# Moving small work off the tensor engine in a fused memory-attention and MLP kernel: w1 in quarters, segment sums on VectorE, a 64-column memory guess, a split last output

## The chip, the cores and the metric

One core of one Trainium2 chip. The metric is the device time of one execution in microseconds (us), as a median over runs. Engine names below: PE is the tensor engine, PEld its weight loads, DVE is VectorE, ACT is ScalarE, POOL is GpSimd, SP is SyncE, which issues most of the DMAs here. The granted clock is the share of its full clock that PE was given, as the profile lists it. L300 means line 300 of the kernel that is spoken of. The two kernels number their lines differently; the few lines that matter are given for both.

## The reference, cut to what matters

Two branches run on a layer-normalised input `xn` (2048 tokens of 1024) and are added. Branch B is an MLP with gelu; branch A is attention with 32 heads over 64 segments of 32 tokens, in which 8 memory rows are handed from each segment to the next:

```python
mem = mem0                                   # 8 rows of 1024
for s in range(64):
    h = concat([mem, xs[s]])                 # 8 + 32 rows
    q, k, v = h @ Wq, h @ Wk, h @ Wv
    o = softmax(mask(q k / sqrt(128))) v @ Wo
    mem = o[:8]                              # the next segment's memory
    out.append(o[8:])
```

This is a chain of 64 steps. The kernel breaks it with a guess. The weights are so small that each softmax is nearly flat, so a memory row is nearly the mean of the segment's values. With `sum_s` the sum of segment s over its tokens (for s = 0 plus the sum of the 8 rows of `mem0`), the guess for the memory after segment s is `(sum_s / 40) @ Wv @ Wo`. All segments are then computed in parallel from the guess. At the end the memory rows that come out are compared with those guessed, 70 rows in all. If one row is off by more than 2^-7 in relative norm, the kernel runs the serial loop of 64 segments after all. The result is right in both cases; only the time differs.

## The kernel before: the parts that matter

Stage 1 (the first MLP product) normalises token tiles, transposes them and multiplies them with w1. Tiles below `NPE` are transposed by PE, the others by ScalarE (normalise) and a DMA transpose. The segment sums are 8 matmuls per tile with a 0/1 matrix of 4 columns:

```python
NPE = 8
...
load_x(0); load_x(1)
for c in range(2):                                     # w1 in halves
    nc.sync.dma_start(w1_sb[:, :, c*512:(c+1)*512], w1_v[:, :, c*512:(c+1)*512])
    load_x(c + 2)
...
def seg_sums(n, xn):                                   # L290
    ps = psum0.tile([P, KT, 4], F32, tag="xs")
    for k in range(KT):
        nc.tensor.matmul(ps[:, k, :], xn[:, k*P:(k+1)*P], segsum[:], start=True, stop=True)
    nc.scalar.copy(xsum[:, :, 4*n:4*n+4], ps[:])
```

The guess is cut into 24 units (8 of Wv, 8 of Wo, 8 of Wv again) that are pushed between the matmuls of the MLP. `mem_start` makes the operand `xb` of the first 8:

```python
def mem_start():
    ...                                                # ps9: mem0 transposed, and its row sum in column M
    nc.vector.tensor_tensor(t0[:], ps9[:, :, M:M+1], xsum[:, :, 0:1], op=ALU.add)
    nc.vector.tensor_copy(xb[:, :, 8:NQ], xsum[:, :, 1:NSEG])
    nc.vector.tensor_copy(xb[:, :, 0:8], t0[:].to_broadcast((P, KT, 8)))   # NQ = 71 columns

for tb in range(4):                                    # blocks of 512 tokens
    for f in range(28):
        ... 8 matmuls with w3 (L523), gelu on ScalarE
        if tb == 0 and f == 20:
            mem_start()
        if tb > 0 and f % 7 == 6:
            spec_step(depth)                           # run one unit
    for j in range(4):
        n = tb * 4 + j
        R1, xt = r1s.pop(n); load_r1(n + 1)            # residual tiles
        ... 56 matmuls with w4 (L548), VectorE adds R1
        if n == 15:
            while pending or units: spec_step(depth)
        elif n > 0:
            spec_step(depth)                           # one unit here too, in block 0 as well
```

## Time and profile before

| | before |
|---|---|
| median | 1530.0 us (1529.5 to 1530.5 in the 4 runs beside the change) |
| span of the profiled run | 1527.2 us |
| first matmul of stage 1 / of the w2 product / of the value projection | 9.5 / 75.1 / 542.6 us |
| last PE matmul starts | 1521.7 us, 5.5 us before the end |

The head of the profile page (busy us, share of the span, number of instructions):

```profile
span 1527.2 us, 24314 instructions
## 1 busy us (share of the span) xinstructions
PE 1512.6 (99%) x9810; PEld 810.3 (53%) x9883; DVE 530.1 (35%) x1131; ACT 506.8 (33%) x1155; POOL 178.8 (12%) x248
```

All waits of PE in the view of waits (engine, tile, line, then what it waited for: us in total, times, longest):

```profile
PE ps L300 <- DMA w_sb<-in_B_w_dram: 2.0, 1, 2.0
PE ps L283 <- DVE xn L264: 1.3, 1, 1.3
PE warm L317 <- DVE wz L311: 1.3, 1, 1.3
PE ps L292 <- DVE xnk L273: 0.7, 1, 0.7
PE ps L300 <- ACT xn2T L287: 0.2, 1, 0.2
PE pso L710 <- issue: 0.2, 1, 0.2
```

PE is never without work for long: the waits sum to 5.7 us, nearly all in the first 20. So time can only come from fewer PE instructions, from the start, or from the tail.

The PE timeline gives the prices (start, length, engine, line, instruction, count). A segment sum (L292) pushes the next matmul back by 24.96 - 24.75 = 0.21 us; a guess unit (L440) takes 243.45 - 242.42 = 1.03 us. The listed length of 1.20 us is longer, as it overlaps the next line by 0.17 us:

```profile
24.75 0.34 PE L292 MATMUL ps<-c_segsum_sb,xnk 128*128 128x4 bf16 x8
24.96 1.25 PE L300 MATMUL ps<-xn2T,w_sb 128*128 128x256 bf16 x10
...
242.42 1.20 PE L440 MATMUL ps<-xb,wt 128*128 128x71 bf16 x32
243.45 2.75 PE L523 MATMUL ps<-xn3T,w_sb 128*128 128x512 bf16 x12
```

And two lines of the view by source line (minimum, median and maximum length in ns, then first and last start in us), the matmuls of `mem_start` (L425), the first guess unit (L440):

```profile
L425 PE MATMUL ps<-c_eye_sb,m x8: 162/162/176, 166.5 to 166.7; 8*128 8x9 bf16 x8
...
L440 PE MATMUL ps<-xb,wt x256: 196/198/198, 203.0 to 295.9; 128*128 128x71 bf16 x128
```

### The profile page before, as it was taken

What the parts mean: (1) busy time and instruction counts of PE and PEld (TensorE: products, weight loads), DVE (VectorE), ACT (ScalarE), POOL (GpSimd) and SP (SyncE); (2) the same over time, 40 slices, a digit from 0 to 9 for tenths busy, and PEclk for the clock granted to TensorE, in tenths of its full rate; (3) what the DMA queues carried; (4) which work ended last, traced back from release to release, by engine and by line L of the source; (5) the groups of instructions that cost most, each with busy time, mean ns of one, the idle gap of its engine ahead of it and who ended that gap; (6) DMA issues with size and microseconds to landing.
All of it is one profiled execution on the core that took longest, in us unless ns stands there. A gap on an engine that the chain in (4) does not pass through costs nothing.

```text
span 1527.2 us, 24314 instructions
## 1 busy us (share of the span) xinstructions
PE 1512.6 (99%) x9810; PEld 810.3 (53%) x9883; DVE 530.1 (35%) x1131; ACT 506.8 (33%) x1155; POOL 178.8 (12%) x248
## 2 busy tenths in 40 slices
PE   8999999999999999999999999999999999999998
PEld 7844444444444444444466645654665555445554
DVE  8284010000210122211146624650664266426641
ACT  5533202103012011111156614650663266326620
POOL 5232020221211222100000010001000100010001
PEclk9999999999999999999999999999999999999999
DMA  8679543452352877632399947992997389728611
GB/s 252 186 221 308 208 158 118 142 183 90 115 176 80 213 259 255 223 123 82 125 242 247 235 133 183 234 244 74 229 251 187 106 222 227 183 80 203 177 46 51
DMA packets 287373, 270.03 MB, mean 177 GB/s; under 512 B 136875, under 2 KB 255040, under 8 KB 287000
## 3 DMA queue, kind: packets, MB, share of 16 engines
q1 hardware_dynamic: 265208, 185.79, 47.5%
q0 software_dynamic: 22048, 82.63, 15.5%
q8 instruction: 80, 1.31, 0.4%
q14 instruction: 37, 0.30, 0.1%
HBM read 190.98 MB, written 46.19 MB: 155 GB/s over the span
## 4 chain that ended last, share of the span: by engine, by line
PE 98%; DMA 1%; DVE 0%; issue 0%; ACT 0%; SPq 0%
PE ps L652 30%; PE ps L579 14%; PE pso L710 14%; PE ps L523 13%; PE ps L548 13%; PE ps L387 4%; PE ps L300 3%; PE psS L667 2%; PE psO L691 2%; DMA xt<-in_A_x_dram 1%; PE ps L474 1%; PE ps L837 1%; PE ps L440 1%; PE gps L454 1%; PE ps L292 0%
## 5 line engine op out<-in xcount | busy, mean ns | idle before, releaser
L652 PE MATMUL ps<-hTb,wt 128*128 128x396 bf16 (+3 forms) x2560 | 509.5, 343 | 0.0
L652 PEld LDWEIGHTS <-wt 128*128 128x128 bf16 x2560 | 234.2, 98 | 166.1
L710 PE MATMUL pso<-wo_sb,oX 128*128 128x512 bf16 x1001 | 223.4, 379 | 1.3 <-issue 0.2
L579 PE MATMUL ps<-wt,xT 128*128 128x512 bf16 x1004 | 220.1, 379 | 1.1
L523 PE MATMUL ps<-xn3T,w_sb 128*128 128x512 bf16 x896 | 195.7, 379 | 0.0
L548 PE MATMUL ps<-w_sb,h3T 128*128 128x512 bf16 x872 | 194.3, 379 | 1.2
L579 PEld LDWEIGHTS <-xT 128*128 128x128 bf16 x1024 | 100.2, 98 | 120.8
L524 ACT ACTIVATE h3T<-ps 128x512 bf16<-128x512 f32 x112 | 66.9, 597 | 292.1 <-PE ps L523 291.2
L710 PEld LDWEIGHTS <-oX 128*128 128x128 bf16 x1024 | 98.8, 98 | 115.3
L658 ACT CAST KT<-ps 128x396 bf16<-128x396 f32 (+3 forms) x160 | 82.3, 514 | 224.0 <-PE ps L652 222.5
L548 PEld LDWEIGHTS <-h3T 128*128 128x128 bf16 x896 | 86.8, 98 | 102.8
L523 PEld LDWEIGHTS <-w_sb 128*128 128x128 bf16 x896 | 86.8, 98 | 102.7
L673 DVE TENSOR_REDUCE sums<-sm 99x4 f32<-99x396 f32 (+2 forms) x176 | 97.6, 555 | 113.4 <-ACT sm L671 113.4
L669 DVE TENSOR_TENSOR sm<-psS,c_mask_reg_sb 99x396 f32<-99x396 f32 x160 | 91.3, 571 | 90.2 <-PE psS L667 89.7
L671 ACT ACTIVATE sm<-sm 99x396 f32<-99x396 f32 (+2 forms) x176 | 92.8, 527 | 71.6 <-DVE sm L669 70.9
L581 ACT CAST Vs<-ps 128x512 bf16<-128x512 f32 x64 | 37.4, 586 | 233.3 <-PE ps L579 169.2
L660 ACT ACTIVATE QT<-ps 128x396 bf16<-128x396 f32 (+3 forms) x160 | 84.2, 526 | 74.0 <-PE ps L652 54.1
L585 DVE CAST Vs<-ps 128x512 bf16<-128x512 f32 x64 | 44.3, 692 | 170.0 <-PE ps L579 157.1
L549 DVE TENSOR_TENSOR R<-ps,R 128x512 f32<-128x512 f32 x32 | 22.1, 692 | 232.0 <-PE ps L548 221.1
L679 DVE TENSOR_TENSOR Pn<-sm,rs 99x396 bf16<-99x396 f32 (+2 forms) x176 | 98.9, 562 | 6.3 <-DVE rs L675 0.5
L692 ACT CAST oX<-psO 128x384 bf16<-128x384 f32 (+1 forms) x176 | 82.4, 468 | 8.3 <-PE psO L691 7.8
L717 POOL DMA_DIRECT2D out_dram<-ot x30 | 16.4, 546 | 583.5 <-DVE ot L716 577.6
(118 smaller groups left out, 978.3 us busy)
## 6 DMA issues: line engine op xcount, KB each, us to landing
wt<-in_A_Wk_dram SPq DMA_DIRECT2D x78, 512.0 KB
wt<-in_A_Wq_dram SPq DMA_DIRECT2D x76, 512.0 KB
wt<-in_A_Wv_dram POOLq DMA_DIRECT2D x24, 1024.0 KB, 6.8
V_scratch<-Vs SPq DMA_DIRECT2D x32, 512.0 KB
V<-V_scratch SPq DMA_DIRECT2D x32, 384.0 KB
w_sb<-in_B_w_dram SPq DMA_DIRECT2D x9, 1024.0 KB
R_scratch<-x POOLq DMA_DIRECT2D x16, 512.0 KB, 3.9
R<-R_scratch SPq DMA_DIRECT2D x16, 512.0 KB
```

The lines of the kernel that those rows point to most:

```text
L523: nc.tensor.matmul(ps[:].rearrange("p (n t) -> p n t", t=P), w3_sb[:, k, f * P:(f + 1) * P], xn3T[tb][:, :, k, :], start=(k == 0), stop=(k ...
L548: nc.tensor.matmul(ps[:], h3T[:, f, j * P:(j + 1) * P], w4_sb[:, f, ch * 512:(ch + 1) * 512], start=(f == 0), stop=(f == FT - 1))
L579: nc.tensor.matmul(ps[:], xT[:, m4 * 4 + j, k, :], wv[:, k, :], start=(k == 0), stop=(k == KT - 1))
L652: nc.tensor.matmul(ps[:, :nb] if flat else ps[:, :nb].rearrange("p (t c) -> p t c", t=nt), w[:, k, hh * P:(hh + 1) * P], B["rhs"](k), star ...
L658: nc.scalar.copy(o, i)
L660: nc.scalar.mul(o, i, scale)
L669: nc.vector.tensor_tensor(sm[:T, :, :T], S3, t["mask"][:].unsqueeze(1).to_broadcast((T, 4, T)), op=ALU.add)
L671: nc.scalar.activation(e[:T, :, :T], sm[:T, :, :T], ACTF.Exp, scale=LN2)
L673: nc.vector.tensor_reduce(ss, e[:T, :, :T], axis=AX.X, op=ALU.add)
L679: nc.vector.tensor_tensor(Pn[:T, :, :T], e[:T, :, :T], rs[:T, :].unsqueeze(2).to_broadcast((T, 4, T)), op=ALU.mult)
L692: nc.scalar.copy(oX[:, hs_, at:at + nt], O3[:, :, 0:nt])
L710: nc.tensor.matmul(self.ps[:], self.oX[:, h, self.gl * P:(self.gl + 1) * P], wo_sb[:, h, self.cc], start=(h == 0), stop=(h == H - 1))
```

## The change

The intent, in four parts: (1) start earlier, with w1 in four column quarters, and take the transposes of tiles 4 to 7 off PE (`NPE = 4`); (2) take the 128 segment-sum matmuls off PE: reload `xn` from its DRAM scratch with DMA transposes while w3 runs, and sum on VectorE; (3) compute the guess on 64 columns, not 71, as the first 8 are equal; (4) produce the last output tile in two halves of 256 columns, so that less is left to evict after the last matmul.

```diff
-                    NPE = 8
+                    NPE = 4
@@ start
                     load_x(0)
-                    load_x(1)
-                    for c in range(2):
-                        w1 half c; load_x(c + 2)
-                    for n in range(4, 7):
+                    for c in range(4):
+                        w1 quarter c
+                        if c < 2:
+                            load_x(c + 1)
+                    for n in range(3, 7):
                         load_x(n)
@@ warm-up matmuls: 13 -> 15; norm_stats(1, 0) now after norm2(0)
@@ MLP phase: the PE version of seg_sums is gone, and
+                def seg_sums(n):
+                    xr = ring.tile([P, KT, P], BF16, tag="xr")          # 2 buffers
+                    nc.sync.dma_start_transpose(xr[:], xn_v[:, n, :])
+                    nc.vector.tensor_reduce(xb[:, :, 4*n:4*n+4], xr[:]..., axis=AX.X, op=ALU.add)
                 def mem_start():
                     ...
-                    nc.vector.tensor_tensor(t0[:], ps9[:, :, M:M+1], xsum[:, :, 0:1], op=ALU.add)
-                    nc.vector.tensor_copy(xb[:, :, 8:NQ], xsum[:, :, 1:NSEG])
-                    nc.vector.tensor_copy(xb[:, :, 0:8], t0[:].to_broadcast((P, KT, 8)))
+                    nc.vector.tensor_tensor(xb[:, :, 0:1], ps9[:, :, M:M+1], xb[:, :, 0:1], op=ALU.add)
@@ in the loop over blocks
-                        if tb == 0 and f == 20:
+                        if tb == 0 and f >= FT - NT:
+                            seg_sums(f - FT + NT)
+                        if tb == 1 and f == 0:
+                            m0s = [ring.tile([M, D], BF16, tag="xr", name="m0")]
+                            nc.sync.dma_start(m0s[0][:], A_mem0[0])
+                        if tb == 1 and f == 3:
                             mem_start()
@@ guess units: NQ -> NSEG columns; GT rows 0 to 6 are copies of column 0; 72 -> 71 in the third set
@@ outputs: the last Out of 512 columns becomes two of 256; the last three stores go to the SP queue
```

More of the change, by code (lines that the diff above doesn't have):

```diff
@@ L125 @@
     ident = const_tile("c_ident", np.eye(P, dtype=np.float32))
-    segsum_np = np.zeros((P, 4), np.float32)
-    for t in range(P):
-        segsum_np[t, t // SEG] = 1.0
-    segsum = const_tile("c_segsum", segsum_np)
     eye9 = const_tile("c_eye9", np.concatenate([np.eye(M, dtype=np.float32), np.ones((M, 1), np.float32)], 1))
@@ L192 @@
             w3ctx = bctx.enter_context(ExitStack())
-            xctx = bctx.enter_context(ExitStack())
-            xsum = xctx.enter_context(tc.tile_pool(name="xs", bufs=1)).tile([P, KT, NSEG], BF16)
             w3_pool = w3ctx.enter_context(tc.tile_pool(name="w3", bufs=1, side="right"))
@@ L228 @@
                     load_x(0)
-                    load_x(1)
-                    for c in range(2):
-                        nc.sync.dma_start(w1_sb[:, :, c * 512:(c + 1) * 512], w1_v[:, :, c * 512:(c + 1) * 512])
-                        load_x(c + 2)
-                    for n in range(4, 7):
+                    for c in range(4):
+                        nc.sync.dma_start(w1_sb[:, :, c * 256:(c + 1) * 256], w1_v[:, :, c * 256:(c + 1) * 256])
+                        if c < 2:
+                            load_x(c + 1)
+                    for n in range(3, 7):
                         load_x(n)
@@ L287, in transposes @@
                             nc.scalar.copy(xn2T[:, jj, half * 4:half * 4 + 4, :], ps[:])
-                    def seg_sums(n, xn):
-                        ps = psum0.tile([P, KT, 4], F32, tag="xs")
-                        for k in range(KT):
-                            nc.tensor.matmul(ps[:, k, :], xn[:, k * P:(k + 1) * P], segsum[:], start=True, stop=True)
-                        nc.scalar.copy(xsum[:, :, 4 * n:4 * n + 4], ps[:])
                     def stage1(n0, nt, xn2T, between):
@@ L315 @@
                     ps = psum.tile([P, 512], F32, tag="mm", bufs=4, name="warm")
-                    for i in range(13):
-                        nc.tensor.matmul(ps[:], wz[:, :P], wz[:], start=(i == 0), stop=(i == 12))
+                    for i in range(15):
+                        nc.tensor.matmul(ps[:], wz[:, :P], wz[:], start=(i == 0), stop=(i == 14))
                     norm_stats(0)
-                    norm_stats(1, 0)
                     t0 = xn2T_tile()
                     xn2 = norm2(0, t0, 0)
+                    norm_stats(1, 0)
                     transposes(xn2, t0, 0, 0)
@@ L333, in first @@
                         transposes(xn2, t1, 0, 1)
-                    xns = {}
-                    def sums_of(n):
-                        if n in xns:
-                            seg_sums(n, xns.pop(n))
                     stage1(0, 1, t0, {3: [first], 4: [lambda: norm_stats(3)]})
@@ L349, in prep @@
                         for m in done:
-                            xns[m] = norm1(m)
+                            norm1(m)
                     def tr(n, half):
@@ L370 @@
                             between[5] += [lambda m0=m0: prep(m0 + 1)]
-                        between[3] += [lambda n0=n0: sums_of(n0 - 1)]
-                        between[4] += [lambda n0=n0: sums_of(n0 - 2)]
                         stage1(n0, nt, tiles2[n0], between)
-                    for n in range(NT):
-                        sums_of(n)
                 xn3T = [wpool.tile([P, 4, KT, P], BF16, tag="w", name=f"xn3T{tb}") for tb in range(4)]
@@ L410 @@
                 w4_sb = big.tile([P, FT, D], BF16)
-                m0 = ring.tile([M, D], BF16, tag="m0", bufs=1)
-                nc.sync.dma_start(m0[:], A_mem0[0])
                 for _ in range(4):
@@ L416 @@
                     nc.sync.dma_start(w4_sb[:, 4 * c:4 * (c + 1), :], w4_v[:, 4 * c:4 * (c + 1), :])
-                vbT = big.tile([P, H, NQ + 1], BF16)
-                xb = big.tile([P, KT, NQ + 1], BF16)
+                vbT = big.tile([P, H, NSEG], BF16)
+                xb = big.tile([P, KT, NSEG], BF16)
                 gps = []
+                def seg_sums(n):
+                    xr = ring.tile([P, KT, P], BF16, tag="xr")
+                    nc.sync.dma_start_transpose(xr[:], xn_v[:, n, :])
+                    with nc.allow_low_precision(reason="sums are accumulated in fp32 and rounded once"):
+                        nc.vector.tensor_reduce(xb[:, :, 4 * n:4 * n + 4], xr[:].rearrange("p k (s t) -> p k s t", t=SEG), axis=AX.X, op=ALU.add)
                 def mem_start():
+                    m0 = m0s[0]
                     ps9 = psum3.tile([P, KT, M + 1], F32, tag="vr")
@@ L426, in mem_start @@
                     nc.vector.tensor_copy(MZ[:, :, 0:M], ps9[:, :, 0:M])
-                    t0 = ring.tile([P, KT, 1], F32, tag="t0", bufs=1)
-                    nc.vector.tensor_tensor(t0[:], ps9[:, :, M:M + 1], xsum[:, :, 0:1], op=ALU.add)
-                    nc.vector.tensor_copy(xb[:, :, 8:NQ], xsum[:, :, 1:NSEG])
-                    nc.vector.tensor_copy(xb[:, :, 0:8], t0[:].to_broadcast((P, KT, 8)))
+                    nc.vector.tensor_tensor(xb[:, :, 0:1], ps9[:, :, M:M + 1], xb[:, :, 0:1], op=ALU.add)
                 def unit_vb(hg):
@@ L436, in run @@
                     def run():
-                        ps = psum3.tile([P, 4, NQ], F32, tag="vr")
+                        ps = psum3.tile([P, 4, NSEG], F32, tag="vr")
                         for hh in range(4):
                             for k in range(KT):
-                                nc.tensor.matmul(ps[:, hh, :], wv[:, k, hh * P:(hh + 1) * P], xb[:, k, :NQ], start=(k == 0), stop=(k == KT - 1))
-                        nc.vector.tensor_scalar(vbT[:, hg * 4:(hg + 1) * 4, :NQ], ps[:], 1.0 / L, None, op0=ALU.mult)
+                                nc.tensor.matmul(ps[:, hh, :], wv[:, k, hh * P:(hh + 1) * P], xb[:, k, :], start=(k == 0), stop=(k == KT - 1))
+                        nc.vector.tensor_scalar(vbT[:, hg * 4:(hg + 1) * 4, :], ps[:], 1.0 / L, None, op0=ALU.mult)
                     return run
@@ L449, in run @@
                         if c == 0:
-                            gps.extend(psum3.tile([P, 4, NQ], F32, tag="g", name=f"gps{i}") for i in range(2))
+                            gps.extend(psum3.tile([P, 4, NSEG], F32, tag="g", name=f"gps{i}") for i in range(2))
                         for hh in range(4):
@@ L453, in run @@
                             for k in range(KT):
-                                nc.tensor.matmul(gps[k // 4][:, k % 4, :], wo[:, hh, k * P:(k + 1) * P], vbT[:, h, :NQ],
+                                nc.tensor.matmul(gps[k // 4][:, k % 4, :], wo[:, hh, k * P:(k + 1) * P], vbT[:, h, :],
                                                  start=(h == 0 and k % 4 == 0), stop=(h == H - 1), skip_group_check=True)
@@ L457, in run @@
                             for i in range(2):
-                                nc.vector.tensor_copy(GT[:, 4 * i:4 * i + 4, :], gps[i][:])
+                                nc.vector.tensor_copy(GT[:, 4 * i:4 * i + 4, 7:NQ], gps[i][:])
+                                nc.vector.tensor_copy(GT[:, 4 * i:4 * i + 4, 0:7], gps[i][:, :, 0:1].to_broadcast((P, 4, 7)))
                             nc.vector.tensor_copy(MZ[:, :, M:NQ + 1], GT[:, :, 7:NQ])
@@ L473, in run @@
                             for k in range(KT):
-                                nc.tensor.matmul(ps[:, hh, :NQ + 1], wv[:, k, hh * P:(hh + 1) * P], MZ[:, k, :], start=(k == 0), stop=(k == KT - 1))
+                                nc.tensor.matmul(ps[:, hh, :NQ], wv[:, k, hh * P:(hh + 1) * P], MZ[:, k, :NQ], start=(k == 0), stop=(k == KT - 1))
                         vrs = vrs2[hg % 2]
-                        nc.vector.tensor_copy(vrs[:, :, :NQ + 1], ps[:, :, :NQ + 1])
+                        nc.vector.tensor_copy(vrs[:, :, :NQ], ps[:, :, :NQ])
                         vrt = ring.tile([P, 4, P], BF16, tag="vrt")
                         nc.sync.dma_start_transpose(vrt[:], vrs[:].rearrange("p h r -> p (h r)"))
-                        nc.sync.dma_start(Vr_d[:, hg * 512:(hg + 1) * 512].rearrange("r (h e) -> r h e", e=DH), vrt[:NQ + 1])
+                        nc.sync.dma_start(Vr_d[:NQ, hg * 512:(hg + 1) * 512].rearrange("r (h e) -> r h e", e=DH), vrt[:NQ])
                     return run
@@ L557 @@
                         nc.gpsimd.dma_start(R_v[:, n, :], R1[:])
-            xctx.close()
             vsp = vctx.enter_context(tc.tile_pool(name="vsp", bufs=3, side="right"))
@@ L698, with __init__ @@
         class Out:
-            def __init__(self, oX, gi, gl, ch):
-                self.oX, self.gi, self.gl, self.cc, self.ps = oX, gi, gl, slice(ch * 512, (ch + 1) * 512), None
+            def __init__(self, oX, gi, gl, c0, w=512):
+                self.oX, self.gi, self.gl, self.cc, self.ps, self.w = oX, gi, gl, slice(c0, c0 + w), None, w
                 self.late = self.last = False
@@ L707, in piece @@
                     self.Rt = iop.tile([P, 512], F32, tag="Rt")
-                    nc.gpsimd.dma_start(self.Rt[:], R_v[:, self.gi, self.cc])
+                    nc.gpsimd.dma_start(self.Rt[:, :self.w], R_v[:, self.gi, self.cc])
                 for h in range(4 * hg, 4 * hg + 4):
-                    nc.tensor.matmul(self.ps[:], self.oX[:, h, self.gl * P:(self.gl + 1) * P], wo_sb[:, h, self.cc], start=(h == 0), stop=(h == H - 1))
+                    nc.tensor.matmul(self.ps[:, :self.w], self.oX[:, h, self.gl * P:(self.gl + 1) * P], wo_sb[:, h, self.cc], start=(h == 0), stop=(h == H - 1))
                 if hg == 7:
@@ L713, in piece @@
                     if DEBUG_A:
-                        nc.vector.tensor_copy(ot[:], self.ps[:])
+                        nc.vector.tensor_copy(ot[:, :self.w], self.ps[:, :self.w])
                     else:
-                        nc.vector.tensor_tensor(ot[:], self.ps[:], self.Rt[:], op=ALU.add)
-                    (nc.sync if self.last else nc.gpsimd).dma_start(out_v[:, self.gi, self.cc], ot[:])
+                        nc.vector.tensor_tensor(ot[:, :self.w], self.ps[:, :self.w], self.Rt[:, :self.w], op=ALU.add)
+                    (nc.sync if self.last else nc.gpsimd).dma_start(out_v[:, self.gi, self.cc], ot[:, :self.w])
         smalls = []
@@ L810 @@
                     smalls.append((due, ("S", gi_), s_item))
-            outs = [Out(oXs[B["b"]], 3 * B["b"] + gl, gl, ch) for B in Bs for gl in range(4 if B["b"] == 4 else 3) for ch in range(2)]
+            outs = [Out(oXs[B["b"]], 3 * B["b"] + gl, gl, ch * 512) for B in Bs for gl in range(4 if B["b"] == 4 else 3) for ch in range(2)]
+        o = outs.pop()
+        outs += [Out(o.oX, o.gi, o.gl, c0, 256) for c0 in (512, 768)]
         head, rest = outs[:4], outs[4:]
@@ L816 @@
             o.late = True
-        for o in rest[-2:]:
+        for o in rest[-3:]:
             o.last = True
```

## The prediction

> **What bounds the kernel.** The tensor engine: PE is busy 1512.6 of 1527.2 us (page, part 1), and 98% of the chain of waits is PE. Its waits in all: 1.3 us for the first memset, 1.3 for the first normalised tile (L283), 2.0 for w1 (L300), 0.7 for the first segment sum (L292). After the last matmul (about 1522.1) some 5 us of eviction and store follow. Only removed PE instructions, the start and the tail can pay. VectorE is 35% busy, but 4.8 of each 5 us from 15 to 30 us (windows).
>
> **Costs, from start-to-start times in the PE timeline.**
> - Segment sums: 8 matmuls of 4 columns take 0.205 us (25.6 ns each), 16 times: 3.3 us removed. The replacement, 16 DMA transposes and 16 VectorE reductions (about 1.2 us each, estimated from 0.555 us for 396 elements), falls at 145 to 175 us, where VectorE is idle (3.1 of 50 us busy): free.
> - Transposes of tiles 4 to 7 leave PE: 8 matmuls of 56 ns per tile, 1.8 us.
> - Memory guess: 32 matmuls of 71 columns take 1.03 us (32.2 ns each). [...]
> - Last output: eviction of 256 instead of 512 columns, 0.69 to about 0.37 us, a smaller last store; short matmuls cost 0.1 us more. Net 0.4 us.
> - Start: 0.75 instead of 1.5 MB lie ahead of the first L300 matmul, so the 2.0 us wait should mostly vanish, with part of the slow clock (mean 0.66 from 10 to 15 us). But x1 now lies behind a w1 quarter and delays VectorE[...]; and x3 still lies behind 3 MB (it arrived at 13.56 us), and tile 2 is normalised only after x3's statistics (about 16 us). The early gain is mostly lost by then.
>
> **The new wait.** Tiles 4 and 5 now go through ScalarE and a DMA transpose on the SP queue. In program order tile 5's transpose stands behind the loads of x9 to x11, which wait for the kept copies of tiles 2 to 4 on VectorE (about 24.3 us by present durations); with 0.75 us per load and 1.3 us per transpose issue it lands at about 28.5 us. PE would be ready for group (4,5) at about 26.8 us: a wait of 1 to 2 us on xn2T. Before, that group started at 28.9 us. So almost nothing is gained until there; after it the remaining sums and transposes are won: 4.3 us for stage 1 as a whole (5.1 us removed and 3 us of start waits shortened, the rest given back in the new wait).
>
> **Sum.** 4.3 + 1.6 + 0.4 = 6.3 us: 1523.8 us, 0.4% faster. 8 in 10: 1520.0 to 1527.0. Faster by over 2%: 0.01; within: 0.98; slower: 0.01.
>
> **What would show it.** Right: L300's wait for w1 below 1 us; a PE wait on xn2T at 26 to 29 us; first L387 matmul at about 71 instead of 75.1 us; a guess unit 0.94 instead of 1.03 us; no PE wait at the new reductions; last matmul to end 0.4 us shorter. Wrong: no wait at group (4,5) and L387 at 68 to 69 us (total about 1521), or over 4 us of wait there (about 1526).
>
> **What would make it wrong.** Transposes landing late among the w2 and x loads; [...]the scratch transposes delaying MLP loads; the memory guess failing its check, which runs the serial loop (far slower).

Cut above is what did not come from the traces of this case: two clauses, and the working of one term of the sum, the 1.6 us for the guess units. The sum was 4.3 + 1.6 + 0.4 = 6.3 us, its 1.6 made of 1.5 us for 64 instead of 71 columns and 0.1 us for the third set. The profile of before gives the same 1.5 us (estimate): 56 matmuls of 256 columns take 70.58 - 64.47 = 6.11 us (L300), 109.1 ns each, against 32.2 ns at 71 columns, so 0.416 ns a column, 2.9 ns for 7 columns, 512 times. The other sizes beside what the profiles show: four transposes start to start 0.22 us (L283), 55 ns each. A reduction of 1024 elements, forecast at 1.2 us, took 1.22 us in the changed kernel (L404). The eviction of 256 columns, forecast at 0.37 us, took 0.42 us in the changed kernel (L703).

## The result, and the profile after

The changed kernel takes 7310.8 us (7307.8 to 7317.1, 4 runs), against 1530.0 for the kernel before in the same rounds: 4.78 times, interval 4.77 to 4.79. The result is correct. Here and below a ratio is the mean time of one kernel's fast runs over that of the other's of the same rounds, so not quite the ratio of the medians.

The head of the page, and two groups of its fifth part (busy us, mean ns | idle before and releaser):

```profile
span 7314.9 us, 134351 instructions
...
PE 5489.9 (75%) x58141; PEld 3019.1 (41%) x58141; DVE 1568.5 (21%) x3194; ACT 1220.1 (17%) x3055; POOL 179.5 (2%) x252
...
L905 PE MATMUL ps<-wv,hseg 128*40 128x512 bf16 x4096 | 1418.2, 509 | 163.0 <-DMA wv<-in_A_Wv_dram 163.0
L940 PE MATMUL ps<-wo_sb,oTs 128*40 128x512 bf16 x4096 | 1154.2, 430 | 33.0 <-ACT oTs L934 33.0
```

L905 and L940 lie inside the serial loop. It ran: the check of the guess failed. The windows before and after the end of the main part (length, then busy us of PE, PEld, DVE, ACT and POOL with their counts, granted clock, DMA share, GB/s):

```profile
0.00:1542.00 1542.00, 1515.12 (x9757) 807.80 (x9757) 545.93 (x1144) 505.63 (x1135) 179.50 (x252) 1.00 0.67 178
1542.00:7314.00 5772.00, 3974.74 (x48384) 2211.28 (x48384) 1022.60 (x2050) 714.42 (x1920) 0.00 (x0) 0.77 0.90 283
```

So 5772 us are the loop, and the main part ends at about 1542 us, not at the 1524 predicted. There are two things to explain, a large one and a small one. These lines answer to the two source lines of before, `mem_start` (L410 now) and the first eight units (L422 now):

```profile
L410 PE MATMUL ps<-c_eye_sb,m x8: 162/162/175, 254.2 to 254.4; 8*128 8x9 bf16 x8
...
L422 PE MATMUL ps<-xb,wt x256: 192/193/242, 218.4 to 312.7; 128*128 128x64 bf16 x128
```

Before, `mem_start` preceded the first unit by 36 us. Now it follows it by 36 us, and the PE timeline has three units ahead of it, at 218.4, 233.3 and 246.3 us. Each covers 4 heads, so heads 0 to 11 read column 0 of `xb` without the sum of `mem0`.

The waits of PE in the main part, longest first:

```profile
PE ps L422 <- DVE xb L404: 11.1, 1, 11.1
PE ps L288 <- DMA xn2T<-xn: 4.3, 2, 2.7
PE ps L566 <- ACT Vs L568: 2.6, 1, 2.6
PE ps L288 <- ACT xn2T L281: 2.5, 3, 1.9
PE ps L277 <- DVE xn L258: 2.4, 3, 1.1
...
PE ps L288 <- DMA w_sb<-in_B_w_dram: 0.6, 1, 0.6
```

The wait for w1 shrank from 2.0 to 0.6 us, as predicted. New are 11.1 us of the first unit for the VectorE sums (L404) and some 7 us in stage 1 (the lines of L288). Two of these waits cost more than their length, since the granted clock fell with them: 0.57 from 24 to 28 us (the 1.9 us for L281), 0.50 from 218 to 222 us. After the two for DMA transposes (2.7 and 1.6 us) it was 1.00. The w2 product starts at 79.3 us instead of 75.1; I had said 71.

Why the sums are late is in the SP queue's timeline:

```profile
157.84 2.92 SPq L393 DMA_DIRECT2D w_sb<-in_B_w_dram  x1
160.80 2.58 SPq L497 DMA_DIRECT2D R<-R_scratch  x1
163.43 0.43 SPq L498 DMA_DIRECT2D xr<-in_A_x_dram  x1
163.90 51.05 SPq L402 DMA_TRANSPOSE xr<-xn_scratch  x16
215.01 0.57 SPq L497 DMA_DIRECT2D R<-R_scratch  x1
```

The 16 transposes stand in program order behind the loads of w3, w4 (L393) and of the first residual tile. They are issued from 163.9 us on, and take 51.05 / 16 = 3.2 us each on average. That is no pure transpose time: the view of the queue's waits has 26.3 us of waiting in it, 11.7 of them until VectorE freed one of the two buffers. The sums end here (VectorE timeline; the 1.22 us each are as estimated):

```profile
175.78 2.35 DVE L404 TENSOR_REDUCE xb<-xr 128x32 bf16<-128x1024 bf16 x2 [39.08 <-DMA xr<-xn_scratch]
...
217.09 1.22 DVE L404 TENSOR_REDUCE xb<-xr 128x32 bf16<-128x1024 bf16 x1 [0.64 <-DMA xr<-xn_scratch]
```

The last ends at 218.3, the unit starts at 218.36. The load of the second residual tile (L497, at 215.01) also stands behind the 16 transposes; that will matter below.

### The profile page after: what moved, and what is told of

It reads as the page before. It is cut to its first block, busy times and chain, and to the rows that moved or that the text cites. A ratio compares the mean times of both kernels' runs of the same rounds, so it can differ in the third digit from the quotient of the medians.

```text
span 7314.9 us, 134351 instructions
## 1 busy us (share of the span) xinstructions
PE 5489.9 (75%) x58141; PEld 3019.1 (41%) x58141; DVE 1568.5 (21%) x3194; ACT 1220.1 (17%) x3055; POOL 179.5 (2%) x252
## 5 line engine op out<-in xcount | busy, mean ns | idle before, releaser
L905 PE MATMUL ps<-wv,hseg 128*40 128x512 bf16 x4096 | 1418.2, 509 | 163.0 <-DMA wv<-in_A_Wv_dram 163.0
L940 PE MATMUL ps<-wo_sb,oTs 128*40 128x512 bf16 x4096 | 1154.2, 430 | 33.0 <-ACT oTs L934 33.0
L906 DVE CAST Va<-ps 40x512 bf16<-40x512 f32 x512 | 349.6, 683 | 3057.7 <-PE ps L905 3057.7
L905 PEld LDWEIGHTS <-hseg 128*40 128x40 bf16 x4096 | 482.0, 124 | 874.7 <-issue 467.0
L896 PE MATMUL ps<-hseg,wq 128*128 128x40 bf16 x16384 | 558.5, 189 | 367.1 <-DMA wq<-in_A_Wq_dram 366.6
L901 PE MATMUL ps<-hseg,wk 128*128 128x40 bf16 x16384 | 525.5, 184 | 405.3 <-DMA wk<-in_A_Wk_dram 403.6
L896 PEld LDWEIGHTS <-wq 128*128 128x128 bf16 x16384 | 504.6, 103 | 519.6 <-issue 381.2
L901 PEld LDWEIGHTS <-wk 128*128 128x128 bf16 x16384 | 471.1, 98 | 520.4 <-DMA wk<-in_A_Wk_dram 449.7
L940 PEld LDWEIGHTS <-oTs 128*40 128x40 bf16 x4096 | 403.2, 111 | 506.8 <-issue 221.2
L697 PE MATMUL pso<-wo_sb,oX 128*128 128x512 bf16 (+1 forms) x1056 | 225.2, 373 | 0.0
L566 PE MATMUL ps<-wt,xT 128*128 128x512 bf16 x1024 | 221.3, 379 | 2.6 <-ACT Vs L568 2.6
```

Source lines behind the costliest of these rows:

```text
L566: nc.tensor.matmul(ps[:], xT[:, m4 * 4 + j, k, :], wv[:, k, :], start=(k == 0), stop=(k == KT - 1))
L697: nc.tensor.matmul(self.ps[:, :self.w], self.oX[:, h, self.gl * P:(self.gl + 1) * P], wo_sb[:, h, self.cc], start=(h == 0), stop=(h == H - 1))
L896: nc.tensor.matmul(ps[:, hh, :], wq[:, k, hh * P:(hh + 1) * P], hseg[:, k, :], start=(k == 0), stop=(k == KT - 1))
L901: nc.tensor.matmul(ps[:, hh, :], wk[:, k, hh * P:(hh + 1) * P], hseg[:, k, :], start=(k == 0), stop=(k == KT - 1))
L905: nc.tensor.matmul(ps[:L, :], hseg[:, k, :], wv[:, k, :], start=(k == 0), stop=(k == KT - 1))
L906: nc.vector.tensor_copy(Va[:, cs_], ps[:L, :])
```

## The experiments

### Why the loop runs: four kernels

Theory ORDER: the three early units read column 0 too soon. Rival ROUNDING: the 32-term sum with a bf16 output is not accumulated in fp32 as the code's comment claims, so many rows miss the tolerance. The rival is a serious one. I emulated the guess and one attention pass on the reference's own inputs, on a host, in three ways, and compared the relative distance of guessed and resulting memory rows with the tolerance 2^-7 = 0.0078:

```
variant                                          first memory's rows   largest other   rows failing
sums exact, then bf16                            0.0037                0.0036          0
sums accumulated in bf16                         0.0079                0.0084          21
sums exact, heads 0 to 11 without sum(mem0)      0.0160                0.0036          8
```

Both theories make the check fail, but with 8 and with 21 failing rows. (The emulation is no run on the chip. Its 0.0079 lies just above the tolerance, so the 21 is soft; the 0.0160 of the 8 rows is twice the tolerance.) This gives a test on the chip: the number of failing rows, plus a count of softmax sums that are out of range, is what the branch reads.

**mem_first.** The three units are held back to block 1.

```diff
-                        elif n > 0:
+                        elif tb > 0:
                             spec_step(depth)
```

> The changed kernel with one word altered: the three guess units that ran between the output tiles of the first token block are held back to the second block, so that the sum of the initial memory is added to column 0 before any unit reads it. Theory ORDER (three units, heads 0 to 11, read column 0 without the initial memory; the check then fails and the serial loop runs): no loop, about 1525 to 1533 us, and the 11.1 us wait of the guess matmuls for the reductions is gone. Rival ROUNDING (the 32-term sum with a bf16 output is accumulated in bf16, so many rows miss the tolerance): the loop still runs, about 7300 us.

Measured: 1577.3 us (1570.5 to 1584.8, 4 runs), ratio 1.029 (1.026 to 1.032); correct. No loop, with the VectorE sums unchanged: ROUNDING falls. But the time is 44 us above the upper end of what I expected. The longest wait of PE in its profile is

```profile
PE ps L566 <- ACT Vs L568: 37.0, 1, 37.0
```

at the turn to the value projection. That is taken up below.

**before_late.** The kernel before, with only the addition of `mem0` moved behind the three units. (`xb` is filled with the sums at the old place, since otherwise the units would read a tile that nobody has written; a memory check before the run refuses that. In the changed kernel the VectorE sums write column 0, so the tile is written and the check has nothing to say: the value is only incomplete.)

```diff
                         if tb == 0 and f == 20:
-                            mem_start()
+                            nc.vector.tensor_copy(xb[:, :, 8:NQ], xsum[:, :, 1:NSEG])
+                            nc.vector.tensor_copy(xb[:, :, 0:8], xsum[:, :, 0:1].to_broadcast((P, KT, 8)))
+                        if tb == 1 and f == 3:
+                            mem_start()
```

> The kernel before, its segment sums still by the tensor engine in fp32, with only the addition of the initial memory moved behind the first three guess units. ORDER: the serial loop runs, about 7310 us. ROUNDING: the sums are those of before, so no loop, about 1530 us.

Measured: 7282.9 us (one run). The order alone produces the loop, with sums by the tensor engine.

**count_over_8** and **count_over_7.** The changed kernel, with another threshold of the branch.

```diff
-    with tc.If(cond > 0):
+    with tc.If(cond > 8):        # count_over_7: cond > 7
```

> The changed kernel as it is, but the loop runs only when more than 8 of the 70 memory rows fail. ORDER: exactly the 8 rows of the first memory are wrong (an emulation of the arithmetic on a host gives 8 failing rows at twice the tolerance), so no loop; the time is that of the changed kernel's main part, about 1543 us, which the profile of the changed kernel shows ending near 1542 us. The result may be slightly wrong, on purpose. ROUNDING: the emulation gives 21 failing rows, so the loop runs, about 7310 us.

> The same with more than 7. ORDER: 8 rows fail, the loop runs, about 7310 us. Fewer than 8 failing rows would give about 1543 us and speak against both theories.

Measured: count_over_8 takes 1548.8 us (1543.1 to 1553.4, 4 runs), ratio 1.011 (1.008 to 1.013), no loop; count_over_7 takes 7308.9 us (one run). The count is exactly 8, as ORDER says; that these are the 8 rows of the first memory is taken from the emulation, since the branch reads only the number. count_over_8 is also the changed kernel's main part with a time of its own, and it is 18.6 us slower than before. (It is not a kernel to keep: it accepts a wrong guess.)

### Why the main part is slower

**mem_block0.** `mem_start` right ahead of the first unit, all unit slots as in the changed kernel.

```diff
-                        if tb == 1 and f == 0:
+                        if tb == 0 and f == FT - 1:
                             m0s = ...                  # load mem0
-                        if tb == 1 and f == 3:
-                            mem_start()
@@ after output tile n
                         elif n > 0:
+                            if n == 1:
+                                mem_start()
                             spec_step(depth)
```

> The changed kernel with the initial memory's addition placed right ahead of the first guess unit, between the first and the second output tile of block 0; the unit slots stay where they were. ORDER: no loop. The wait of the first guess matmuls for the late VectorE reductions (11.1 us in the changed kernel, 15.9 in count_over_8) stays, as in count_over_8, and so does the loss in stage 1: about 1540 to 1550 us. A second theory, that the 37 us wait of mem_first at the turn to the value projection comes from the shift of the last units, says that this wait is absent here (below 5 us).

Measured: 1550.4 us (1547.1 to 1553.7), ratio 1.014. No loop. The waits of PE in its profile begin with:

```profile
PE ps L410 <- DMA m<-in_A_mem_dram: 8.1, 1, 8.1
```

The wait has moved from the units to `mem_start`: the load of `mem0` uses a buffer of the transposed tiles and stands behind them. A wait of 37 us as in mem_first is absent (its wait at L566 is 2.5 us). So the order alone is mended at no gain; the sums are simply not ready at the slots in block 0.

**five_slots.** mem_first, with five unit slots in each of the later blocks, so that the units that were held back are done in time.

```diff
-                        if tb > 0 and f % 7 == 6:
+                        if tb > 0 and f % 5 == 4:
```

> mem_first with five unit slots instead of four in each later block, so that all units are again done before the last output tile. SHIFT theory (the 37 us wait of mem_first is the late last units holding up the queue of loads and the release of buffers): that wait is gone, the reductions have until block 1, so only the loss of stage 1 is left: about 1529 to 1536 us. If the wait stays, something else in the changed kernel causes it, and the time stays near 1570 us.

Measured: 1536.1 us (1531.6 to 1537.7), ratio 1.003 (1.001 to 1.005). The 37 us are gone, which explains mem_first. In mem_first two of the last units ran only at 550 us, after the last MLP tile. The waits of POOL there show what hung on them: the first load into memory that the MLP phase gives up waited for the units' last store to DRAM,

```profile
POOL wo_sb L560 <- DMA Vmem_scratch<-vrt: 36.8, 1, 36.8
```

and so did the value projection's copies on ScalarE and VectorE (they sat idle until 601.6 us). Those stores stood in the SP queue behind transposes of tokens for the next phase; four of them alone held the queue for 25.5 us (563.1 to 588.6 in its timeline). Three postponed units of 1 us each thus cost 37 us of PE, since a memory region was released late. (That it is this chain is read from the trace; the run shows only that the wait goes with the postponed units.) The waits left in five_slots:

```profile
PE ps L288 <- DMA xn2T<-xn: 5.2, 1, 5.2
PE ps L536 <- DVE R L537: 3.6, 1, 3.6
PE ps L277 <- DVE xn L258: 3.3, 4, 1.1
PE ps L288 <- ACT xn2T L281: 2.5, 3, 1.9
```

The second line is new: VectorE adds the residual late, because POOL gets the second residual tile late, because its load stands behind the 16 scratch transposes (in the changed kernel it was issued at 215.01 us, see above). It costs more than its 3.6 us. The window of five_slots after that wait has a granted clock of 0.79:

```profile
222.00:230.00 8.00, 7.69 (x28) 3.12 (x28) 2.14 (x4) 0.00 (x0) 3.28 (x3) 0.79 0.48 163
```

In quarters_only (below) the same wait was 1.91 us and the windows around it keep a clock of 1.00. But the clock also fell after shorter waits than the 3.59 us of five_slots: in npe4_only (below) after 3.06 us at the same place, and in pre_new_8 (below) after 2.02 us at the start of the value projection. The windows after these two waits, in this order:

```profile
222.00:226.00 4.00, 3.85 (x12) 1.43 (x12) 0.69 (x2) 0.00 (x0) 2.71 (x2) 0.63 0.32 131
550.00:554.00 4.00, 3.71 (x10) 1.44 (x11) 0.39 (x1) 1.10 (x3) 4.00 (x5) 0.60 1.02 344
```

The length of a wait alone does not tell whether the clock falls. In the 4 us from the end of a wait it was 0.50 after 11.1 us and 0.63 after 1.89 us in the changed kernel (from 218.36 and 24.80 us), and 0.65 after 2.04 us in the kernel before (from 9.55 us). But it was 1.00 after 2.73, 2.59 and 1.56 us in the changed kernel (from 35.67, 568.11 and 44.38 us). So a wait of about 2 to 3 us is worth its own time in one place and, by 0.4 x 4 us, some 1.6 us more in another (estimate, from the clocks of 0.60 to 0.65).

**five_slots_old_start.** five_slots with the start and the `NPE = 8` of the kernel before; sums on VectorE, 64 columns and split output stay.

```diff
-                    NPE = 4                            # and the order of loads,
+                    NPE = 8                            # 13 warm-up matmuls and the order
                                                        # of norm_stats(1, 0) as before
```

> five_slots with the start of the kernel before: w1 in halves, 13 warm-up matmuls, the old order of the first statistics, and the transposes of tiles 4 to 7 on the tensor engine. START theory (the loss of stage 1, 4.2 us at the first L387 matmul where I had expected a gain of 4, comes from the transposes of tiles 4 to 7 leaving the tensor engine and the changed start): about 8 us faster than five_slots, 1522 to 1528 us, and stage 1 ends at about 71 us, as the segment sums are still gone from it. If the loss came from the segment sums' move, it would stay.

Measured: 1529.3 us (1528.6 to 1538.9), ratio 1.001 (0.998 to 1.005). 6.8 us better than five_slots, so most of the stage 1 loss is in the start and the transposes. Stage 1 ends at 73.6 us in its profile, not at the 71 expected. And it only equals the kernel before, and one run of four stands 9 us above the others.

**guess64_tail.** The kernel before with only the 64 columns and the two halves (edits as in the change; `mem_start` stays at its old place, and writes `xb` from `xsum`).

> The kernel before with only the 64-column guess and the last output in two halves; segment sums on the tensor engine, initial memory at its old place. By the arithmetic of the prediction 1.6 + 0.4 us less than before: 1528.2 us, no loop, a guess unit 0.94 instead of 1.03 us. If the 64-column guess itself were wrong, the loop would run.

Measured: 1530.2 us (1528.3 to 1532.1), ratio 0.999 (0.998 to 1.001): the same, where 2 us less were expected. The gains are there: from the w2 product to the value projection its profile takes 541.4 - 75.4 = 466.0 us, against 542.6 - 75.1 = 467.5 before, and from the check's product to the end 1530.1 - 1489.7 = 40.4 against 1527.2 - 1485.7 = 41.5 us. But the profiled run is one of its upper ones, and has a wait of 2.5 us at the start of the value projection that the profile of before has not. Its runs lie at 1528.3, 1528.4, 1532.0 and 1532.1; those of before on the same chip at 1528.9 to 1529.9 and 1531.2 to 1532.1. A gain of 1 to 2 us is smaller than the step between these two levels (3.6 us here). What decides between them stays open. One candidate: after its wait of 2.5 us the profiled upper run has a clock of 0.57 from 550 to 554 us, so wait and clock together are worth about 4.2 us (estimate: 2.5 + 0.43 x 4), and the mean clock is 0.997 and 0.998 in its two upper runs, 0.999 and 1.000 in the lower ones. But no lower run of it was profiled, and the mean clocks of before do not separate its two levels (0.997 to 0.999 and 0.998).

**npe4_only, quarters_only, npe10_prefetch.** Parts of the start alone, and a try at a faster kernel.

```diff
 # npe4_only: five_slots_old_start with      # quarters_only: five_slots_old_start with
-                    NPE = 8                 -  w1 in halves, 13 warm-ups, old statistics
+                    NPE = 4                 +  w1 in quarters, 15 warm-ups, new statistics
 # npe10_prefetch: five_slots_old_start with NPE = 10 and
                 load_r1(0)
+                load_r1(1)                  # ahead of the 16 scratch transposes
@@
-                        load_r1(n + 1)
+                        if n:
+                            load_r1(n + 1)
```

> five_slots_old_start with only the transposes of tiles 4 to 7 taken off the tensor engine again (w1 in halves, old order). It splits the 6.8 us between five_slots (1536.1) and five_slots_old_start (1529.3). Theory TRANSPOSE (ScalarE normalises tiles 4 and 5 in order, ahead of the copies that PE waits for, and their DMA transposes land late): most of the loss is here, about 1533 to 1536 us, with waits of 1.5 us or more on ScalarE's xn2T and 3 us or more on the DMA's xn2T. Theory START (quarters of w1 put x1 late): nothing here, about 1529 us.

> five_slots_old_start with only the new start: w1 in quarters, 15 warm-up matmuls, the statistics of tile 1 behind the normalisation of tile 0; tiles 4 to 7 transposed by the tensor engine. TRANSPOSE: within 1.5 us of five_slots_old_start, about 1528 to 1530 us. START: about 1535 us.

> A try at a kernel that beats both: five_slots_old_start with tiles 8 and 9 also transposed by the tensor engine and the second residual tile loaded ahead of the 16 scratch transposes. If the waits left in five_slots_old_start (2.6 us on DMA transposes in stage 1, 1.2 us on VectorE behind a late residual) come from these two causes, 2 to 3 us go and 0.9 us of transposes come: about 1527.5 us. If the DMA transposes limit stage 1 by their rate (about 3.6 us each from 42 to 57 us, where two are needed each 7 us), the wait stays and the time is 1529 to 1530 us.

Measured: npe4_only 1536.6 us (1531.8 to 1539.3); quarters_only 1537.9 us, with one run at 1527.3 and four from 1537.1 to 1540.3; npe10_prefetch 1529.4 us (1526.7 to 1532.6, 5 runs), ratio 1.000. The first two did not separate the theories, since both seemed to lose 7 to 8 us. Two levels 10 us apart in one kernel showed that something else was at work, and the profile of quarters_only, which fell on its quick run, names a candidate, the residual (L536 waiting for L537):

```profile
PE ps L277 <- DVE xn L258: 2.7, 4, 1.1
PE ps L536 <- DVE R L537: 1.9, 1, 1.9
```

npe10_prefetch, the only one with the early residual, had no upper level and no such wait. Its time is the one forecast for a limit by the rate of the DMA transposes, and 1.8 of the 2.6 us of wait for them are left. But its profile also has a wait of 3.0 us for w1, with a clock of 0.65 and 0.50 from 8 to 16 us, so it does not settle that.

**pre_old_8, pre_new_8, pre_old_4, pre_new_4.** The two by two of start (old, new) and `NPE` (8, 4), all with the early residual of the diff above.

> quarters_only with the second residual tile loaded ahead of the 16 scratch transposes. Its runs had two levels, 1527.3 and 1537 to 1540 us. RESIDUAL theory (VectorE's addition waits for the late residual, PE waits for VectorE, 1.9 us in the quick profile, and [...]the clock also falls, 0.79 in five_slots): the upper level is gone, 1523 to 1527 us in all runs, clearly below the kernel before. If the upper level has another cause, it stays.

> The same early residual in five_slots_old_start. RESIDUAL: the outlier of 1538.9 us is gone and the profile has no PE wait on L537; about 1527 to 1529 us. Against pre_new_8 it prices the new start alone: the stage 1 profiles (72.8 against 73.6 us) say about 1 us for the new start.

> The same in five_slots, which is then the changed kernel with its two flaws of the guess mended. TRANSPOSE: stage 1 still ends at 78 to 79 us, so about 5 us above pre_new_8: 1529 to 1532 us. START: as pre_new_8.

> The same in npe4_only. TRANSPOSE: stage 1 ends near 79 us, about 5 us above pre_old_8: 1531 to 1534 us. START: as pre_old_8, 1527 to 1529 us.

Measured, medians in us on one chip, with before at 1530.2 (1529.6 to 1532.3):

| | old start | new start (quarters) |
|---|---|---|
| tiles 4 to 7 transposed by PE | 1529.3 (1526.6 to 1532.3) | 1528.8 (1525.1 to 1532.2) |
| tiles 4 to 7 by ScalarE and DMA | 1533.2 (1530.0 to 1537.0) | 1532.5 (1528.2 to 1533.4) |

The transposes cost 3.7 to 3.8 us with either start; the new start gains 0.6 to 0.7 us, which is within the spread. The profiles say the same of the end of stage 1, the first w2 matmul (L366). With tiles 4 to 7 on PE (pre_new_8) and off it (pre_new_4):

```profile
L366 PE MATMUL ps<-w_sb,hTB x250: 379/379/379, 75.0 to 130.0; 128*128 128x512 bf16 x125
L366 PE MATMUL ps<-w_sb,hTB x250: 379/379/379, 78.9 to 134.0; 128*128 128x512 bf16 x125
```

With the old start it is 74.9 (pre_old_8) and 80.5 us (pre_old_4). The upper level of quarters_only is gone: no run of pre_new_8 is above 1532.2, though its runs also miss the forecast of 1523 to 1527 us. TRANSPOSE holds as far as the 2 x 2 goes, START falls, and RESIDUAL is supported. No profile of an upper run of quarters_only exists, so that it was the clock there is inferred from five_slots; the mean clocks fit it (0.996 to 0.998 in the four upper runs, 1.000 in the quick one, worth some 3 to 6 us by estimate). The two kernels ran in different jobs on different chips. pre_new_8 is the best of all, with 0.9984 of before (0.9970 to 0.9998): 0.16%. pre_new_4 is the changed kernel with the guess and the residual mended: it equals before (1.001, 0.999 to 1.002).

Why the DMA transposes of tiles 4 and 5 cost is read from the traces; no run separates the parts. One part is in the ACT timeline of the changed kernel:

```profile
22.87 1.24 ACT L260 ACTIVATE xn<-xt,nm,rr 128x1024 bf16<-128x1024 bf16 x1 [0.61 <-POOL nm L252]
...
24.17 0.58 ACT L281 CAST xn2T<-ps 128x512 bf16<-128x512 f32 x1
```

The copy that PE needs next (L281, the transposed tile 3) stands behind the normalisation of tile 5 (L260), which waits for that tile's statistics and then takes 1.24 us. The copy started at 24.17 us, when that normalisation was over (22.87 + 1.24 = 24.11), and PE waited 1.9 us for it. But after it PE still had to wait 2.7 us for the DMA transposes of the next group, (4,5), which started at 35.7 us instead of about 28.9 before. So it is their landing that set this start; a faster copy alone would only have made the second wait longer. The chain of work in pre_new_4, which has the same kind of wait (4.6 us), shows how long the landing took (view --critical; start, length, what):

```profile
24.68 10.06 DMA xn2T<-xn
```

The transpose was issued at 24.7 us and landed 10.06 us later. In five_slots, npe4_only and pre_old_4 it took 10.60, 10.03 and 10.36 us. In pre_new_8 and pre_old_8, where the first group with DMA transposes is (8,9), it took 8.81 and 9.36 us, but these were issued at 36.5 and 37.5 us, when less work was left to be held up. Why a landing takes so long, next to the loads of x and w2, was not tested.

### The sum of the main part

From the medians, step by step. The medians of the kernel before agree to 0.3 us between jobs, but the runs of each of the other kernels spread over 5 to 10 us, so a step is good to about 2 us:

| step | us |
|---|---|
| before to pre_old_8: sums off PE, 64 columns, split output, units in new slots | -0.8 |
| pre_old_8 to pre_new_8: start in quarters | -0.6 |
| pre_new_8 to pre_new_4: tiles 4 to 7 off PE | +3.7 |
| pre_new_4 to five_slots: late residual | +3.6 |
| five_slots to count_over_8: units waiting for late sums in block 0 | +12.6 |
| sum: before to count_over_8 (1530.2 to 1548.8) | +18.6 |

The first step should have been about -5 by the prediction's prices (3.3 + 1.6 + 0.4). In the profile of pre_old_8 the w2 product starts at 74.9 us, 0.2 earlier than before, though 3.3 us of sums are gone. Its waits in stage 1 are 3.3 us for w1 and 3.0 us for DMA transposes, against 2.0 and none before. With less PE work in stage 1 the transposes by DMA are no longer ready in time, and the gain goes into that wait. That the rate of these transposes is the new limit of stage 1 is likely but was not tested alone.

## Why the prediction was wrong, point by point

- **The guess.** The step that failed is the treatment of the guess as a mere number of columns, "Memory guess: 32 matmuls of 71 columns take 1.03 us", with the failing of its check named only under "What would make it wrong" and given hardly any chance (0.01 for slower by over 2%). The change moved the producer of column 0 (`mem_start`) from block 0 to block 1, but left three of its consumers in block 0. In its place the runs showed: the order alone makes the loop run (before_late), mending it stops the loop (mem_first, mem_block0), and exactly 8 rows fail (count_over_8 and count_over_7). It could have been predicted with certainty from the program order of PE, where L422 precedes L410. This step is 5762 us (7310.8 - 1548.8) of the 5787 (7310.8 - 1523.8) by which the prediction was off.
- **"falls at 145 to 175 us, where VectorE is idle ... free."** Wrong by place, not by size. A sum took 1.22 us, as estimated. But the transposes queue behind the weight loads, and the sums ran from 175.8 to 218.3 us. I asked whether VectorE was free and not when its input would arrive, nor who in the same queue would then be late: 11.1 us of wait, and the late residual besides.
- **"The new wait"**: right in kind, wrong in size. The mis-sized term is "it lands at about 28.5 us". Tile 5's transpose was issued at 25.8 us, but group (4,5) began only at 35.7, when it had landed: about 10 us after its issue, where 28.5 would have been 2.7. "Transposes landing late among the w2 and x loads" stood among the risks, without a size. PE's own wait was 2.7 us and not more only because PE was late as well: ScalarE had run the normalisation of tile 5 (22.87 us) before the copy of tile 3 (24.17 us), which I had not looked at. L387 "at about 71" was 79.3.
- **"4.3 us for stage 1 as a whole"** was the term mis-sized by most in the main part besides the units: it measured -4.2 us. The landing of the transposes above is most of it, as all the work of groups (4,5) to (14,15) stands behind it.
- **Start**: the wait for w1 fell below 1 us (0.6), as predicted, and the early gain was mostly lost, as predicted (0.6 us net).
- **Guess unit**: 0.94 us predicted. Measured in the PE timeline of quarters_only:

```profile
235.86 1.10 PE L422 MATMUL ps<-xb,wt 128*128 128x64 bf16 x32
236.80 1.46 PE L506 MATMUL ps<-xn3T,w_sb 128*128 128x512 bf16 x6
```

  236.80 - 235.86 = 0.94 us, 29.4 ns per matmul, against 32.2 ns at 71 columns: the forecast was good.
- **Tail**: 0.4 us predicted; from the start of the last matmul to the end it is 4.3 us in count_over_8 against 5.5 before, so 1.2 us.

## What to carry to other kernels

When a change moves the making of an operand, list every instruction that reads it, in program order, and see that each comes after; a memory check does not see a read of a value that has been written but is not complete, least of all where a fallback keeps the result right. Work moved to an idle engine is free only if its input is there in time and its DMAs do not stand in front of others in the same queue (here the sums took 1.22 us each as estimated, yet PE waited 11.1 us for them in the changed kernel, and 3.6 us in five_slots for the residual behind their transposes): look for the queue, not only for the engine. And print the number that a fallback branches on, or make it decide at two thresholds: that number told two theories apart that both predicted the same slow time.
